# Two layers of linear attention and MLP on one core: settled instruction orders and buffers arranged anew, two tiles transposed by DMA, b1 and b2 loaded later, last tile in 384 + 128 columns

## The chip, the core and the metric

The kernel runs on one core of a Trainium2 chip. A core has five engines with instruction streams of their own: PE (matmuls, and the loading of their weights, PEld), DVE (vector work), ACT (functions of one input, with tables that must be switched between exponential and GELU), POOL (general vector work, slower) and SP, which here only issues DMAs. They wait for each other by semaphores alone. PE writes to PSUM, eight banks of 512 float32 columns by 128 rows; everything else lives in SBUF, 128 rows.

The metric is the device time of a run in microseconds (us), the median of several runs. A few lines of a profiled execution show where it goes.

## The reference

The input is 2048 rows of 512 numbers in bfloat16. Two equal layers follow each other, each a linear attention with 32 heads of 16 and an MLP of width 1792, with residual adds:

```python
def _A_ref(x, wqkv, wo):
    q, k, v = ...                          # x @ wqkv, 32 heads of 16
    phi = lambda t: jnp.where(t > 0, t + 1, jnp.exp(t)) + 1e-6
    pq, pk = phi(q), phi(k)
    kv = jnp.einsum("bhsd,bhse->bhde", pk, v)
    z = jnp.einsum("bhsd->bhd", pk)
    num = jnp.einsum("bhqd,bhde->bhqe", pq, kv)
    den = jnp.einsum("bhqd,bhd->bhq", pq, z)[..., None] + 1e-6
    return (num / den) @ wo                # heads side by side
def _B_ref(x, w1, b1, w2, b2):
    y = _layernorm(x)
    return gelu(y @ w1 + b1) @ w2 + b2
x = x + _A_ref(_layernorm(x), A_wqkv, A_wo)
x = x + _B_ref(_layernorm(x), B_w1, B_b1, B_w2, B_b2)
x = x + _A_ref(_layernorm(x), A_wqkv, A_wo)
x = x + _B_ref(_layernorm(x), B_w1, B_b1, B_w2, B_b2)
```

## The kernel before

The 2048 rows are 16 tiles of 128 rows, in four groups of four. Counting tiles from one, "tile five" is tile 4 in the names. The names in the order lists are those of the code: the first digit behind a letter is the layer, 0 or 1, then the tile or the group and the part.

First stage, for each tile: `norm` (L755) takes mean and variance on DVE (statsA0, aggrA0; for tile 3 by two ACT passes, sumA0_3 and sqA0_3), adds epsilon (vepsA0, DVE or POOL), raises to -1/2 on POOL (powA0) and writes the normalised tile on DVE or ACT (normA0). The tile is then turned, columns to rows, either by `transpose_pe` (L808: four PE instructions PTA0 of 128 columns into a PSUM bank, then a copy tcA0 by ACT) or by `transpose` (L800: one DMA on SP's queue, TA0). `attn_k` makes the keys (K0, four matmuls of 512 columns) and `phi` (L834) their features by an exponential on ACT (expk0), a second pass (reluk0) and work on DVE (mink0) and DVE or POOL (phik0). `attn_g_held` sums tile-transposed times features over all tiles in four PSUM banks (G0), `attn_z` sums the features (Z0, sixteen one-column matmuls for a group), `attn_q` makes the queries (Q0) and their features.

Then V and the output weights are folded into the sum (`attn_kv`: KV0, kvm, M0, cpm), the denominators are made (`attn_den`: D0 with ln and rec on ACT for the first two groups; pz, red, den, rec on POOL and DVE for the other two, with pr multiplying the query features and TP turning them by DMA), and `attn_out` multiplies (WO0) and adds the residual on DVE (RA0). `mlp_front` normalises (normB0), turns the tile (TB0 by DMA) and adds b2 to the residual (b20, POOL or DVE). `mlp_up` makes the hidden layer (W10; group 0 in two halves of 256 columns, the others 512) with GELU on ACT, `mlp_down` sums it (W20, two halves of seven matmuls) and adds the residual (RB0). The second layer does the same with names 1; its key sum goes by groups through `gacc`, its output rows leave by SP's queue (OD). The last tile's down product is made in two column halves (W21_15_h0 and _h1, L1141 to L1159), each with its own PSUM bank, DVE add and output DMA.

Nothing is scheduled when the program is built. `CONF` holds for each engine the whole order of its instructions (ORDER), for each buffer the order in which its tiles use it (PLACES), and for each step that has a choice its way (WAY: which engine, or PE against DMA). `Settled` (L105) takes these, makes every first user of a buffer wait for all users of the tile before it, and `assign_waits` (L186) puts a semaphore wait where an instruction needs one of another engine's. Each engine goes through its list strictly in order. WARM is a list of warm-up blocks at the start of PE's list: matmuls of constants into a PSUM bank, with their columns.

In the order of before, PE starts with 15 warm-ups of 512 columns, then PTA0_0 and PTA0_1, K0_0, PTA0_2, K0_1 and so on. Tiles 0 to 5 are turned by PE, 6 to 15 by DMA. On SP's queue, b2 is loaded between the transposes of tiles 12 and 10, and b1 after the last of them (`dma(..., after=[tr])`, L1193 to L1198, only behind tile 0's transpose by dependence). POOL issues the loads of wv, wo, w1 and w2 once all first-stage transposes are there (`late`, L1205 to L1212).

Of the kernel before, what the change touches and what calls it, by code (L numbers as in the profile page):

```python
# [10 lines left out]
P = 128  # L11
S = 2048
D = 512
# [172 lines left out]
def assign_waits(graph, order, sems, dma_sems):  # L186
# [10 lines left out]
    while len(done) < total:  # L197
        moved = False
        for e in ENGINES:
# [42 lines left out]
    WARM=[[512, 512, 512, 512, 512, 512, 512, 512, 512, 512, 512], [512, 512, 512, 512]],  # L242
# [40 lines left out]
        "act":  # L283
# [1046 lines left out]
```

## Time and profile before

| | us |
|---|---|
| three runs | 328.95, 328.55, 329.53 |
| median | 328.95 |
| the profiled execution | 327.5 |
| its span, first to last instruction | 326.3 |
| granted PE clock in it | 1.000 |

The page of the profile gives the engines' busy time and the chain of work that ended last, followed back from the end. "PE ps L866" is a matmul of line 866 that writes PSUM. In the answers in order of time, a row gives the start, the length and what ran; a bracket at its end tells how long the engine was idle before and what ended that. Rows merge neighbours of one kind, so that "x4" are four instructions. Ends of matmuls are modelled and overlap the next start; the distance of starts is the better measure of their cost.

### The profile page before, as it was taken

How to read it: one execution, taken by the hardware profiler on the slowest of the kernel's cores; microseconds unless marked ns; L12 is line 12 of the kernel's file. 1: busy time of each engine (PE TensorE's matmuls, PEld its weight loads, DVE VectorE, ACT ScalarE, POOL GpSimd, SP SyncE). 2: the span in 40 equal slices, each digit the busy share in tenths (PEclk: the TensorE clock that was granted, in tenths of full speed). 3: DMA queues.
4: the chain of work that ended last, by engine and by line, in shares of the span. 5: the costliest groups of instructions: out<-in, count | busy, mean ns of one | idle time of the engine just before them, and what ended most of it. 6: DMA issues, size and time to landing. Idle time of an engine off the chain costs nothing.

```text
span 326.3 us, 4763 instructions
## 1 busy us (share of the span) xinstructions
PE 322.2 (99%) x1723; PEld 159.3 (49%) x1723; DVE 211.0 (65%) x503; ACT 193.1 (59%) x334; POOL 152.5 (47%) x224
## 2 busy tenths in 40 slices
PE   8999999999999999999999999999999999999997
PEld 3444445576454444444444444458644444444444
DVE  5987679996938685142436899999989983300112
ACT  4988769797661416529673477969833454551600
POOL 5662548588663417300757434783856593100000
PEclk9999999999999999999999999999999999999999
DMA  7355753334012210331011110012034322200102
GB/s 266 120 83 97 219 189 104 105 64 68 16 32 50 54 26 3 80 64 34 0 32 33 34 32 0 19 32 50 17 82 94 69 48 66 64 0 2 64 0 80
DMA packets 46883, 20.37 MB, mean 62 GB/s; under 512 B 41932, under 2 KB 45388, under 8 KB 46860
## 3 DMA queue, kind: packets, MB, share of 16 engines
q1 hardware_dynamic: 44572, 13.00, 18.8%
q0 software_dynamic: 1056, 4.72, 4.5%
q10 hardware_dynamic: 1232, 2.36, 2.0%
q8 instruction: 13, 0.21, 0.3%
q14 instruction: 10, 0.08, 0.1%
HBM read 8.00 MB, written 2.10 MB: 31 GB/s over the span
## 4 chain that ended last, share of the span: by engine, by line
PE 97%; DVE 1%; ACT 1%; issue 0%
PE ps L1127 30%; PE ps L1163 29%; PE ps L1097 9%; PE ps L866 8%; PE ps L883 5%; PE ps L987 4%; PE ps L958 4%; PE ps L896 2%; PE ps L747 2%; PE ps L1150 1%; PE ps L1074 1%; PE ps L1008 1%; PE ps L1031 1%; PE ps L941 1%; PE ps L817 0%; DVE pkb L854 0%
## 5 line engine op out<-in xcount | busy, mean ns | idle before, releaser
L1132 ACT ACTIVATE gT<-ps,b1c 128x512 bf16<-128x512 f32 (+1 forms) x140 | 77.1, 600 | 65.3 <-PE ps L1127 65.0
L1127 PE MATMUL ps<-t,w 128*128 128x512 bf16 (+1 forms) x560 | 102.2, 336 | 0.0
L1163 PE MATMUL ps<-w,gT 128*128 128x512 bf16 x434 | 97.6, 379 | 0.0
L1127 PEld LDWEIGHTS ps<-t,w 128*128 128x128 bf16 x560 | 54.6, 98 | 43.7 <-ACT t L827 0.3
L1163 PEld LDWEIGHTS ps<-w,gT 128*128 128x128 bf16 x434 | 42.5, 98 | 50.4 <-DVE xsb L1169 0.2
L782 POOL TENSOR_TENSOR rstd<-veps,neghalf 128x1 f32<-128x1 f32 x64 | 37.9, 602 | 33.5 <-DVE veps L780 31.4
L837 ACT ACTIVATE eb<-ps 128x512 bf16<-128x512 f32 x64 | 37.4, 614 | 18.3 <-PE ps L866 10.5
L1173 DVE TENSOR_TENSOR outb<-ps,xsb 128x512 bf16<-128x512 f32 x15 | 10.1, 686 | 46.3 <-PE ps L1163 40.3
L773 DVE BATCH_NORM_STATS2 stats<-xsb 128x6 f32<-128x512 f32 x48 | 32.3, 678 | 0.4
L848 ACT ACTIVATE rb<-ps 128x512 bf16<-128x512 f32 x45 | 26.6, 617 | 9.2 <-PE ps L866 8.7
L866 PE MATMUL ps<-wqkv,t 128*128 128x512 bf16 x128 | 31.6, 379 | 0.1
L1097 PE MATMUL ps<-gtb,t 128*128 128x512 bf16 x128 | 31.2, 379 | 0.1
L850 DVE TENSOR_SCALAR eb<-eb 128x512 bf16<-128x512 bf16 x45 | 14.0, 321 | 21.1 <-ACT eb L837 21.1
L1113 POOL TENSOR_TENSOR xsb<-xsb,b2b 128x512 f32<-128x512 f32 x20 | 24.3, 1224 | 6.8 <-ACT yb L790 6.6
L790 ACT ACTIVATE yb<-xsb,nmr,rstd 128x512 bf16<-128x512 f32 x21 | 16.7, 812 | 14.2 <-POOL nmr L787 13.9
L780 POOL TENSOR_SCALAR veps<-mv 128x1 f32<-128x1 f32 x35 | 7.6, 217 | 30.8 <-DVE mv L775 28.1
L1063 POOL TENSOR_TENSOR t<-t,rr 128x512 bf16<-128x512 bf16 x14 | 15.5, 1114 | 13.6 <-DVE rr L1059 12.9
L795 DVE TENSOR_SCALAR yb<-xsb,mv,rstd 128x512 bf16<-128x512 f32 x27 | 16.1, 602 | 8.5 <-POOL rstd L782 8.3
L1051 POOL TENSOR_TENSOR lr<-t,zrow 128x512 f32<-128x512 bf16 x15 | 17.9, 1191 | 5.7 <-ACT zrow L971 4.2
L883 PE MATMUL ps<-wqkv,t 128*128 128x512 bf16 x80 | 19.9, 379 | 0.0
L1097 PEld LDWEIGHTS ps<-gtb,t 128*128 128x128 bf16 x128 | 12.3, 98 | 14.7 <-DVE rr L1059 0.6
L866 PEld LDWEIGHTS ps<-wqkv,t 128*128 128x128 bf16 x128 | 12.0, 98 | 14.9 <-ACT t L827 1.0
(97 smaller groups left out, 373.5 us busy)
## 6 DMA issues: line engine op xcount, KB each, us to landing
w<-in_B_w_dram POOLq DMA_DIRECT2D x4, 896.0 KB, 6.9
out_dram<-outb SPq DMA_DIRECT2D x15, 128.0 KB, 1.9
t<-in_A_x_dram ACTq DMA_DIRECT2D x3, 512.0 KB, 4.6
t<-yb SPq DMA_TRANSPOSE x56, 2.5
wqkv<-in_A_wqkv_dram ACTq DMA_DIRECT2D x1, 512.0 KB, 5.8
wqkv<-in_A_wqkv_dram POOLq DMA_DIRECT2D x1, 512.0 KB, 4.6
wo<-in_A_wo_dram POOLq DMA_DIRECT2D x1, 512.0 KB, 5.5
t<-in_A_x_dram SPq DMA_DIRECT2D x1, 384.0 KB, 3.1
```

The lines of the kernel that those rows point to most:

```text
L773: G.op("dve", lambda e: e.bn_stats(stats[:, s.slot, :], src()), 620, reads=src_keys, writes=[k + "s"], tiles=[s, *src_tiles], name=f"stats ...
L782: G.op("pool", lambda e: e.tensor_tensor(rstd[:, s.slot:s.slot + 1], veps[:, s.slot:s.slot + 1], neghalf[:], op=ALU.pow), 570, reads=[k + ...
L837: G.op("act", lambda e: e.activation(eb[:, et.slot, :], bank(bt), ACT.Exp), 478, reads=[src_key], writes=[f"e{tag}"], tiles=[bt, et], name ...
L848: G.op("act", lambda e: e.activation(rb[:, rt.slot, :], bank(bt), ACT.Relu), 478, reads=[src_key], writes=[f"r{tag}"], tiles=[bt, rt], nam ...
L866: ins = e.matmul(bank(b), lhsT=yTa(yT)[:, dt, k * P:(k + 1) * P], rhs=wqkv[:, dt, D:2 * D], start=(dt == 0), stop=(dt == DT - 1))
L883: ins = e.matmul(bank(b), lhsT=yTa(yT)[:, dt, k * P:(k + 1) * P], rhs=wqkv[:, dt, 0:D], start=(dt == 0), stop=(dt == DT - 1))
L1051: lambda e, r=r, tok=tok: e.tensor_tensor(lr[:, r.slot, :], tok(), zrow[:], op=ALU.mult), 1150 if on_pool else 600,
L1097: ins = e.matmul(bank(wb), lhsT=yTa(pq)[:, kt, k * P:(k + 1) * P], rhs=gtb[:, kt, :], start=(kt == 0), stop=(kt == DT - 1))
L1113: G.op("pool" if on_pool else "dve", lambda e: e.tensor_tensor(xsb[:, st, :], xsb[:, st, :], b2b[:], op=ALU.add), 1120 if on_pool else 600 ...
L1127: ins = e.matmul(bank(b, n), lhsT=w1[:, dt, ft * P:(ft + 1) * P], rhs=yTa(yT)[:, dt, k0 * P:k1 * P], start=(dt == 0), stop=(dt == DT - 1))
L1132: G.op("act", lambda e, ft=ft, b=b, k0=k0, k1=k1, n=n: e.activation(gT[:, g.slot, ft * 512 + k0 * P:ft * 512 + k1 * P], bank(b, n), ACT.Ge ...
L1163: ins = e.matmul(bank(b), lhsT=gT[:, g.slot, ft * 512 + k * P:ft * 512 + (k + 1) * P], rhs=w2[:, ft, :], start=(ft == 0), stop=(ft == FT - 1))
```

## The change

The code changes in four places, and `CONF` is new as a whole.

1. WARM: one block of seven matmuls of 512 columns and ten blocks of 256. PE's order puts five of the ten ahead of the first tile's transposes and five behind, ahead of K0_0.
2. WAY: TA0_4 and TA0_5 from "pe" to "dma"; their PTA0 and tcA0 instructions leave PE's and ACT's lists, and two TA0 join SP's.
3. The DMAs of b1 and b2 and the two POOL instructions of the head mask are made behind the loop over first-stage tiles; the loads now depend on all first-stage transposes, and SP's order has b1, Tb1 and b2 behind the last of them.
4. The last tile's down product is made of columns 0 to 383 and 384 to 511.

ORDER and PLACES are different lists on all five engines. Work moves between DVE and POOL (WAY): of the large sums and products of layer 0, thirteen go from POOL to DVE (b20 of tiles 7, 8, 11, 12, 13; pr0_0_3, pr0_1_2, pr0_2_0, pr0_2_2, pr0_2_3; pz0_2_3, pz0_3_1, pz0_3_3) and six from DVE to POOL (b20 of tiles 2 and 6; pr0_0_2, pr0_1_0, pr0_3_0, pr0_3_1); layer 1 and the small epsilon steps change in the same manner. ACT's order has thirteen switches between the exponential's and GELU's table behind the first, instead of eleven. `norm`, `phi` and `attn_k` get an optional path for a centred tile, which no entry of WAY asks for, so that its code makes no instruction.

```diff
-    WARM=[[512, 512, 512, 512, 512, 512, 512, 512, 512, 512, 512], [512, 512, 512, 512]],
+    WARM=[[512, 512, 512, 512, 512, 512, 512], [256], [256], [256], [256], [256], [256], [256], [256], [256], [256]],
...
         "sp":
-            "x0 x1 wk0 TA0_7 TA0_6 TA0_8 TA0_14 TA0_15 TA0_13 TA0_12 b2 TA0_10 TA0_11 TA0_9 b1 Tb1 TB0_1 TB0_0 TB0_2 TB0_3 "
...
+            "x0 x1 wk0 TA0_4 TA0_5 TA0_6 TA0_14 TA0_7 TA0_10 TA0_8 TA0_12 TA0_13 TA0_9 TA0_15 TA0_11 b1 Tb1 b2 TB0_0 TB0_1 "
...
         "pe":
-            "warm0 warm1 PTA0_0 PTA0_1 K0_0 PTA0_2 K0_1 PTA0_3 K0_2 PTA0_4 G0_0_0 K0_3 K0_4 Q0_0_0 G0_1_0 PTA0_5 Q0_0_1 K0_5 "
-            "G0_2_0 Z0_0 G0_3_0 K0_6 K0_7 K0_8 G0_4_0 Q0_1_2 K0_14 G0_5_0 K0_15 G0_6_0 G0_7_0 Q0_1_0 K0_12 Z0_1 K0_13 K0_10 "
-            "K0_11 K0_9 Q0_1_3 Q0_1_1 Q0_0_3 Q0_0_2 G0_8_0 Z0_3 Z0_2 G0_9_0 G0_10_0 D0_0_0 G0_11_0 G0_12_0 D0_0_2 G0_13_0 "
...
+            "warm0 warm3 warm1 warm10 warm7 warm8 PTA0_0 warm4 warm2 warm9 warm6 warm5 K0_0 PTA0_1 PTA0_2 K0_1 PTA0_3 K0_2 "
+            "K0_3 G0_0_0 Q0_0_1 Q0_0_3 K0_4 Q0_0_0 G0_1_0 G0_2_0 K0_5 G0_3_0 Z0_0 G0_4_0 K0_6 K0_14 Q0_1_2 K0_7 G0_5_0 Q0_1_0 "
+            "G0_6_0 K0_10 K0_12 K0_8 K0_13 G0_7_0 K0_9 Z0_1 K0_15 K0_11 Q0_1_1 G0_8_0 Q0_0_2 Z0_2 Z0_3 G0_9_0 G0_10_0 D0_0_0 "
...
         "dve":
-            "ones statsA0_0 aggrA0_0 vepsA0_0 normA0_0 statsA0_1 aggrA0_1 vepsA0_1 statsA0_2 aggrA0_2 normA0_1 statsA0_4 "
...
+            "ones statsA0_0 aggrA0_0 vepsA0_0 statsA0_1 normA0_0 aggrA0_1 statsA0_2 aggrA0_2 vepsA0_2 normA0_1 normA0_2 "
...
-        "TA0_14": "dma", "TA0_15": "dma", "TA0_2": "pe", "TA0_3": "pe", "TA0_4": "pe", "TA0_5": "pe", "TA0_6": "dma",
+        "TA0_14": "dma", "TA0_15": "dma", "TA0_2": "pe", "TA0_3": "pe", "TA0_4": "dma", "TA0_5": "dma",
...
-                for h in range(2):
+                for h, (c0, c1) in enumerate(((0, 3 * P), (3 * P, D))):
                     hb = b if h == 0 else Tile(psum, f"w{L}_{st}_h", "w")
-                    cs = slice(h * D // 2, (h + 1) * D // 2)
+                    cs = slice(c0, c1)
...
-                if st == 0:
-                    dma("sp", lambda e: e.dma_start(b1r[0:FT, :], B_b1.rearrange("(ft p) -> ft p", p=P)), ["b1r"], name="b1", kb=4,
-                        after=[tr])
-                    dma("sp", lambda e: e.dma_start(b2b[:], bass.AP(B_b2.tensor, B_b2.offset, [[0, P], [1, D]])),
-                        ["b2b"], name="b2", kb=128, after=[tr])
-                    consts()
...
+        dma("sp", lambda e: e.dma_start(b1r[0:FT, :], B_b1.rearrange("(ft p) -> ft p", p=P)), ["b1r"], name="b1", kb=4, after=trs)
+        dma("sp", lambda e: e.dma_start(b2b[:], bass.AP(B_b2.tensor, B_b2.offset, [[0, P], [1, D]])), ["b2b"], name="b2", kb=128, after=trs)
+        consts()
```

PE's end in the two orders, the last lists of DVE and SP:

```
PE before:  W21_9_7 W21_15_h0 W21_11_0 W21_11_7 W21_15_h1
PE after:   W21_15_h0 W21_10_0 W21_10_7 W21_8_0 W21_8_7 W21_9_0 W21_9_7 W21_11_0 W21_11_7 W21_15_h1
DVE before: RB1_10 RB1_8 RB1_9 RB1_11 RB1_15_0 RB1_15_1      SP: OD10 OD8 OD9 OD11 OD15_0 OD15_1
DVE after:  RB1_10 RB1_8 RB1_15_0 RB1_9 RB1_11 RB1_15_1      SP: OD10 OD5 OD8 OD15_0 OD9 OD11 OD15_1
```

More of the change, by code (lines that the diff above doesn't have):

```diff
@@ L783, in norm @@
                  570, reads=[k + "v", "neghalf"], writes=[k + "r"], tiles=[s], name=f"pow{tag}")
+            mean = lambda: stats[:, s.slot, 2:3] if by_act else mv[:, s.slot, 0:1]
+            if centred is not None:
+                yc = Tile(YB, f"yc{tag}")
+                G.op("dve", lambda e: e.tensor_scalar(yb[:, yc.slot, :], src(), mean(), None, op0=ALU.add if by_act else ALU.subtract),
+                     300, reads=[k + "m", *src_keys], writes=[f"yc{tag}"], tiles=[s, yc, *src_tiles], name=f"cen{tag}", lat=40, fast=True)
+                centred.append((yc, f"yc{tag}", s, k + "r"))
             y = Tile(YB, f"y{tag}")
@@ L794, in norm @@
             else:
-                G.op("dve", lambda e: e.tensor_scalar(yb[:, y.slot, :], src(), stats[:, s.slot, 2:3] if by_act else mv[:, s.slot, 0:1],
+                G.op("dve", lambda e: e.tensor_scalar(yb[:, y.slot, :], src(), mean(),
                                                       rstd[:, s.slot:s.slot + 1], op0=ALU.add if by_act else ALU.subtract, op1=ALU.mult),
@@ L832, in yTa, with phi @@
             return t4[:, yT.slot, :].rearrange("p (d s) -> p d s", d=DT)
-        def phi(bt, src_key, dst, dst_key, dst_tiles, tag):
+        def phi(bt, src_key, dst, dst_key, dst_tiles, tag, scaled=None):
             et = Tile(EB, f"e{tag}")
-            G.op("act", lambda e: e.activation(eb[:, et.slot, :], bank(bt), ACT.Exp), 478, reads=[src_key], writes=[f"e{tag}"],
-                 tiles=[bt, et], name=f"exp{tag}", lat=90, table="exp")
-            if eng(f"phi{tag}") == "max":
+            by = (lambda: 1.0) if scaled is None else (lambda: rstd[:, scaled[0].slot:scaled[0].slot + 1])
+            more_tiles, more_keys = ([], []) if scaled is None else ([scaled[0]], [scaled[1]])
+            G.op("act", lambda e: e.activation(eb[:, et.slot, :], bank(bt), ACT.Exp, scale=by()), 478, reads=[src_key, *more_keys],
+                 writes=[f"e{tag}"], tiles=[bt, et, *more_tiles], name=f"exp{tag}", lat=90, table="exp")
+            if eng(f"phi{tag}") == "max" and scaled is None:
                 G.op("dve", lambda e: e.tensor_scalar(eb[:, et.slot, :], eb[:, et.slot, :], 1.0, 1e-6, op0=ALU.min, op1=ALU.add),
@@ L847, in phi @@
             rt = Tile(RB, f"r{tag}")
-            G.op("act", lambda e: e.activation(rb[:, rt.slot, :], bank(bt), ACT.Relu), 478, reads=[src_key], writes=[f"r{tag}"],
-                 tiles=[bt, rt], name=f"relu{tag}", lat=90)
+            G.op("act", lambda e: e.activation(rb[:, rt.slot, :], bank(bt), ACT.Relu, scale=by()), 478, reads=[src_key, *more_keys],
+                 writes=[f"r{tag}"], tiles=[bt, rt, *more_tiles], name=f"relu{tag}", lat=90)
             G.op("dve", lambda e: e.tensor_scalar(eb[:, et.slot, :], eb[:, et.slot, :], 1.0, 1e-6, op0=ALU.min, op1=ALU.add),
@@ L856, in phi, with attn_k @@
                  name=f"phi{tag}", lat=60, fast=not on_pool)
-        def attn_k(L, c, k, yT):
+        def attn_k(L, c, k, yT, key=None, scaled=None):
             st = 4 * c + k
@@ L868, in fn @@
                 return ins
-            G.op("pe", fn, 4 * MM, reads=[f"yT{L}_{st}", "wk"], writes=[f"k{L}_{st}"], tiles=[b, yT],
+            G.op("pe", fn, 4 * MM, reads=[key or f"yT{L}_{st}", "wk"], writes=[f"k{L}_{st}"], tiles=[b, yT],
                  name=f"K{L}_{st}", lat=MM_DRAIN, n=4)
-            phi(b, f"k{L}_{st}", lambda: pkb[:, pk.slot, :], f"pk{L}_{st}", [pk], f"k{L}_{st}")
+            phi(b, f"k{L}_{st}", lambda: pkb[:, pk.slot, :], f"pk{L}_{st}", [pk], f"k{L}_{st}", scaled)
             return pk
@@ L1143, in mlp_down, with fn @@
                 ot = Tile(OUT, f"out{st}")
-                for h in range(2):
+                for h, (c0, c1) in enumerate(((0, 3 * P), (3 * P, D))):
                     hb = b if h == 0 else Tile(psum, f"w{L}_{st}_h", "w")
-                    cs = slice(h * D // 2, (h + 1) * D // 2)
-                    def fn(e, hb=hb, cs=cs):
+                    cs = slice(c0, c1)
+                    def fn(e, hb=hb, cs=cs, n=c1 - c0):
                         for ft in range(FT):
-                            ins = e.matmul(bank(hb, D // 2), lhsT=gT[:, g.slot, ft * 512 + k * P:ft * 512 + (k + 1) * P], rhs=w2[:, ft, cs],
+                            ins = e.matmul(bank(hb, n), lhsT=gT[:, g.slot, ft * 512 + k * P:ft * 512 + (k + 1) * P], rhs=w2[:, ft, cs],
                                            start=(ft == 0), stop=(ft == FT - 1))
                         return ins
-                    G.op("pe", fn, FT * 109.2, reads=[f"g{L}_{c}_{ft}_{k}" for ft in range(FT)] + ["w2"], writes=[f"w{L}_{st}_{h}"],
+                    n = c1 - c0
+                    G.op("pe", fn, FT * (n / 2.4 + 2.5), reads=[f"g{L}_{c}_{ft}_{k}" for ft in range(FT)] + ["w2"], writes=[f"w{L}_{st}_{h}"],
                          tiles=[hb, g], name=f"W2{L}_{st}_h{h}", lat=MM_DRAIN, n=FT)
-                    G.op("dve", lambda e, hb=hb, cs=cs: e.tensor_tensor(outb[:, ot.slot, cs], bank(hb, D // 2), xsb[:, st, cs], op=ALU.add), 340,
-                         reads=[f"w{L}_{st}_{h}", ("x", st)], writes=[f"out{st}_{h}"], tiles=[hb, ot], name=f"RB{L}_{st}_{h}", lat=60)
+                    G.op("dve", lambda e, hb=hb, cs=cs, n=n: e.tensor_tensor(outb[:, ot.slot, cs], bank(hb, n), xsb[:, st, cs], op=ALU.add),
+                         60 + n * 1.06, reads=[f"w{L}_{st}_{h}", ("x", st)], writes=[f"out{st}_{h}"], tiles=[hb, ot], name=f"RB{L}_{st}_{h}", lat=60)
                     dma("sp", lambda e, cs=cs: e.dma_start(rows(out_dram, c)[:, k, cs], outb[:, ot.slot, cs]), [f"od{st}_{h}"],
-                        tiles=[ot], reads=[f"out{st}_{h}"], name=f"OD{st}_{h}", sem=f"d_out_h{h}", kb=64)
+                        tiles=[ot], reads=[f"out{st}_{h}"], name=f"OD{st}_{h}", sem=f"d_out_h{h}", kb=n // 4)
                 return
```

16 lines of the change are left out of this document (12 added, 4 removed), and 486 rows, old and new, of tables (ORDER, PLACES, WAY).

## The prediction

> **What bounds the kernel now.** I read the page first, for the shares, then the busy time by stretches, to see where the engine with the highest share ever pauses, then the chain of work that ended last, in order of time.
>
> ```profile
> span 326.3 us, 4763 instructions
> PE 322.2 (99%) x1723; PEld 159.3 (49%) x1723; DVE 211.0 (65%) x503; ACT 193.1 (59%) x334; POOL 152.5 (47%) x224
> PE 97%; DVE 1%; ACT 1%; issue 0%
> ```
> ```profile
> 0.00:8.00 8.00, 6.96 (x23) 2.61 (x23) 4.42 (x12) 3.39 (x6) 4.56 (x16) 1.00 0.72 264
> 32.00:40.00 8.00, 7.34 (x54) 3.46 (x52) 5.45 (x13) 5.84 (x12) 4.33 (x5) 1.00 0.68 198
> 48.00:80.00 32.00, 32.00 (x204) 19.00 (x202) 28.41 (x67) 28.20 (x54) 24.53 (x29) 1.00 0.40 96
> 240.00:318.00 78.00, 77.87 (x362) 35.17 (x360) 33.20 (x68) 30.38 (x47) 22.44 (x28) 1.00 0.21 50
> ```
>
> The columns of the second view are the stretch, its length, the busy time (and instructions) of PE, its weight loads, DVE, ACT and POOL, PE's granted clock, the DMA engines' share and GB/s. TensorE (PE) is the bound: 97% of the chain, 322.2 of 326.3 us busy, and from 48 to 80 us it doesn't pause at all. Faster work on any other engine buys nothing there. A change of order can only win where PE waits (0.66 us in 32 to 40, 0.13 in 240 to 318), ahead of its first useful matmul, behind its last one, or by taking instructions off PE. It can lose everywhere. The chain shows the two ends and the wait:
>
> ```profile
> 0.84 6.34 PE ps L747 x15
> 7.17 0.24 PE ps L817 x4
> 7.43 0.60 ACT t L827
> 8.09 1.04 PE ps L866 x4
> ...
> 14.28 0.86 PE ps L896 x4
> ...
> 16.00 0.22 PE ps L817 x4
> ...
> 30.82 2.71 PE ps L866 x12
> ...
> 36.16 0.69 DVE pkb L843
> 36.85 1.18 DVE pkb L854
> ...
> 39.16 0.29 DVE eb L841
> 39.45 0.34 DVE pkb L854
> 39.84 0.55 PE ps L941 x16
> ...
> 322.61 1.54 PE ps L1150 x14
> 324.17 0.42 DVE outb L1155
> ```
>
> Four 512-column matmuls take 0.86 us (0.216 each), but the fifteen warm-ups 6.34 (0.42 each): until about 7 us PE runs at half rate, though the granted clock of that stretch reads 1.00.
>
> **The change part by part: the start.** The warm-ups shrink from fifteen of 512 columns to seven of 512 and ten of 256, and five of the ten stand behind the first tile's transposes. The other engines decide what that is worth:
>
> ```profile
> 3.21 0.69 DVE L773 BATCH_NORM_STATS2 stats<-t 128x6 f32<-128x512 bf16 x1 [1.75 <-DMA t<-in_A_x_dram]
> 4.99 0.41 DVE L795 TENSOR_SCALAR yb<-t,mv,rstd 128x512 bf16<-128x512 bf16 x1 [0.68 <-POOL rstd L782]
> 8.34 0.38 DVE L795 TENSOR_SCALAR yb<-t,mv,rstd 128x512 bf16<-128x512 bf16 x1
> 10.35 0.41 DVE L795 TENSOR_SCALAR yb<-t,mv,rstd 128x512 bf16<-128x512 bf16 x1
> ```
> ```profile
> 4.42 0.63 ACT L764 ACTIVATE eb<-t 128x512 bf16<-128x512 bf16 x1 [2.34 <-DMA t<-in_A_x_dram]
> 5.53 0.72 ACT L768 ACTIVATE eb<-t,stats 128x512 bf16<-128x512 bf16 x1 [0.39 <-POOL stats L766]
> ```
>
> Before, tile one is normalised at 5.40 (4.99 + 0.41), and its transposes wait for the warm-ups until about 7. After, the second tile's statistics (0.69, from the landing at 4.42) go ahead of that normalise, so it ends near 5.5. The warm-ups ahead of the transposes end at 0.84 + 7 x 0.42 + 5 x 0.21 = 4.85. PE then idles some 0.65, transposes from 5.5 to 5.95 (0.22 doubled by the half rate), runs the other five (1.05) to 7.0, and the copy on ACT (0.60 from about 6.0) is done by then. The first key product starts near 7.0 instead of 8.09.
>
> Not all of these 1.1 us last. The third tile's normalise moves from 8.34 to about 7.3, but the squares of tile four (0.72) now stand behind the first copy, ahead of the second, which is so ready near 8.75. Second key product 8.8, third 9.9, fourth 10.75, first G product 11.6, then two query products that now stand here (they fill the time in which tile five's transposed block arrives): 7 groups of four done by about 14.35 on the chain's scale, where the chain of before has 6 at 14.28. That is 0.86 - 0.07 = 0.8 ahead. Bounds: 0.3 (the copy of each tile again paces PE as before) and 1.1.
>
> **Tiles five and six by DMA.** Eight PE transposes leave; the first four lie in the count above, the other four are the 0.22 at 16.00. Two copies leave ACT. Two transposes join the SP queue and land on their own:
>
> ```profile
> L804 SPq DMA_TRANSPOSE t<-yb x56: 1188/1265/2193, 15.3 to 278.6; - x56
> DMA to landing us min/median/max: 2.4/2.5/4.3
> ```
>
> Tile five's normalise ends near 10.7 (before: 10.35 + 0.41), so its block is there at 13.3, and its key product stands at 14.2: cover 0.9. At the longest landing (4.3) it would wait 0.9. Tile six: normalised near 14.1 (POOL now builds half a mask ahead of its reciprocal root), landed 16.6, used at 14.2 + 4 x 0.86 = 17.6: cover 1.0. Twelve transposes at 1.27 each keep SP busy for 15 us; begun at 10.7 and waiting for some normalises they end by 24 to 29, and the last block is used by PE 21 groups and a z product behind 14.2, at some 33. I take nothing for the queue and 0.22 for the four transposes.
>
> **b1 and b2.** Their loads leave the middle of the transposes; b1, its transpose and then b2 follow once the last block has landed, near 30. Their users, the first GELU and the adds of b2, stand behind the whole key-value part, near 60 by the count of groups between. Nothing, either way.
>
> ```profile
> wqkv<-in_A_wqkv_dram POOLq DMA_DIRECT2D x1, 512.0 KB, 4.6
> ```
>
> The loads of the late weights now stand on POOL behind one more sum of query features, which is fed by a query product that ends near 35 and done at about 39. The V weights, first of them, would land near 39 + 4.6 = 43.6 and are used near 47 by the count of groups: cover 3. Nothing, and up to a few us if that sum is late by more.
>
> **The wait at 33 to 40.** From 30.82 to 39.84 the chain holds 9.02 us; PE's work in it is 36 matmuls (7.78) and a z product (0.38), so 0.86 is waiting. The last key products feed sums whose second half is late on DVE (the rows 36.16 to 39.45). After, the last key product is followed by a query, a G, a query and a z product, 2.6 + 0.38, and its own path is exponential and relu (0.60 each, ACT's time for 512 columns), minimum (0.29), sum (0.34) and one more 0.69: 2.5 us. So it just fits. I take 0.7 of the 0.86; bounds 0.2 (DVE again spends 1.18 on a sum) and 0.86.
>
> **The last tile.** 256 + 256 columns become 384 + 128: PE's sum stays (0.0555 per 128 columns, by the transposes' 0.22 for four), and the work behind the last matmul shrinks.
>
> ```profile
> 322.65 0.69 DVE L1173 TENSOR_TENSOR outb<-ps,xsb 128x512 bf16<-128x512 f32 x1 [2.71 <-PE ps L1163]
> ```
> ```profile
> out_dram<-outb SPq DMA_DIRECT2D x15, 128.0 KB, 1.9
> out_dram<-outb SPq DMA_DIRECT2D x2, 64.0 KB, 1.7
> ```
>
> 0.42 for 256 and 0.69 for 512 columns make about 0.29 for 128: 0.13 less. But the last full tile's output now leaves only 0.78 us of PE ahead of the end and lands 1.9 after its issue, about when the last piece does. I take 0.1; bounds 0 and 0.3.
>
> **Everything between 40 and 318.** The order is new on all engines, so waits can come up anywhere. Two more switches of ACT's function table and 13 heavy sums and products of layer one that go from POOL to DVE, against 6 the other way, lie beside PE's work. The order of before loses nothing in 48 to 80, 0.13 us in 240 to 318 and 0.66 in 32 to 40; I take 0.4 for the new one, between the last two.
>
> Sum: 0.8 + 0.22 + 0.7 + 0.1 - 0.4 = 1.4 us gained. The profiled execution took 327.5 us (span 326.3, 1.2 around it) and lies 1.45 below the median of the runs, 328.95. It becomes 326.1, and the median 328.95 - 1.4 = **327.5**. With all lower bounds and 0.66 lost: 0.3 + 0.2 - 0.66 and the 0.22, a gain of 0.1; with all upper ones 1.1 + 0.22 + 0.86 + 0.3 - 0.13 = 2.35. The forecast's own range is 326.6 to 328.9.
>
> **Rivals.** *PE stays at half rate.* Before, the rate doubled after 6.3 us of unbroken matmuls. After, they are unbroken for only 4.0 us, then comes a gap of 0.65. For: if the gap restarts the count, the rate doubles near 5.5 + 6.3 = 11.8. Against: within 0.84 to 7.0 PE still works nine tenths of the time. Price: from 7.0 to 11.8 work goes at half rate, 2.4 us of it lost, some 0.9 hidden in the waits for copies: 1.5. Gain -0.1, so 329.05, no change.
> The Trainium skill's page "TensorE: Matmul & The Clock Gate", Part 1, has the rate doubled after one busy window of about 3.4 us, with windows that don't start with the kernel, so that the point varies. The 6.3 us of this trace lie within two such windows. By that rule the doubling may come before 7.0 or after 10, by chance, and the sum would be 1.4 or near nothing.
>
> *DVE becomes the bound in 48 to 80* (the other side). There it is busy 28.41 of 32 us, 89%. Of the moved instructions five of those that join DVE and two that leave it fall into this stretch, net 3 more:
>
> ```profile
> L1113 DVE TENSOR_TENSOR xsb<-xsb,b2b 128x512 f32<-128x512 f32 x12 | 11.9, 999 | 0.0
> ```
>
> At 0.69 to 1.0 each (this group shows that a sum from SBUF takes longer than one from PSUM) they add 2.1 to 3.0: 31.0 us. If DVE keeps its 89%, because its idle time is waits for others, the stretch takes 34.8 us, 2.8 longer. It starts 1.7 earlier, so PE leaves it 1.1 later than before; less 0.1 at the end, plus the 0.4: +1.4, 330.35. It decides once PE's second half of the first four tiles has to wait for its normalised blocks. Counted from the first output product, that half stands 18.4 us later (6 single matmuls, 11 groups of four, 14 half-wide groups, seven matmuls); the DVE instructions up to the second of its normalises, the SP issue and the landing come to about 17.8. The cover is 0.6. Against: the POOL waits that DVE sat through get shorter when POOL has less to do, and the third and fourth tile of that group come earlier in DVE's order.
>
> *Tile five late.* At the longest landing of 4.3, and with tile six behind it, PE waits 0.9 in the start: 328.4. Against: 2.5 is the median, and nothing heavy but weights is loading then.
>
> **How the numbers follow.** Forecast 0.54, half rate 0.16, DVE 0.22, late tile 0.08. This kernel's runs tell a change from none beyond 0.3%, about 1 us: faster means under 327.96, slower over 329.94. The forecast is faster in four of five, the late tile in one of four, half rate in one of four (a part of the price): 0.43 + 0.02 + 0.04, and with the upper half of the start's bounds 0.5. DVE is slower in three of four, half rate in one of eight, the forecast hardly: 0.2. The rest, 0.3, is no change. For eight in ten the range runs from 326.5 to 330.3: it leaves out half of the DVE case and the forecast's luckiest end.
>
> **What would show it.** Right: first key product near 7.0; the z products near 37 without a DVE wait ahead of them; PE full from 40 to 318; one 384-column and one 128-column group at the end with about 0.3 us of DVE behind. Wrong: key products of 1.7 instead of 0.86 us near 8 (half rate); PE idle behind the first residual adds, with DVE as releaser, between 60 and 80; a wait of PE for a transposing DMA near 14.

## The result, and the profile after

| | median | runs | lowest, highest |
|---|---|---|---|
| before | 328.9 us | 4 | 328.55, 329.53 |
| after | 326.11 us | 4 | 325.69, 327.05 |

The ratio is 0.9917, with a 95% interval from 0.9889 to 0.9944: 2.8 us faster. The forecast was 1.4 us faster (327.5), with a range from 326.5. The sign was right, and the gain shows at the start, near 40 us and at the end, where it was forecast; its size was twice the forecast, and just outside the range.

The page of the kernel after, and its busy time by the stretches that the prediction used (columns as there):

```profile
span 325.8 us, 4716 instructions
PE 319.6 (98%) x1686; PEld 159.5 (49%) x1717; DVE 214.5 (66%) x522; ACT 194.3 (60%) x334; POOL 134.6 (41%) x205
PE 93%; ACT 3%; DMA 1%; DVE 1%; issue 1%; SPq 0%
```
```profile
0.00:8.00 8.00, 5.96 (x22) 2.88 (x23) 3.96 (x12) 3.11 (x6) 3.56 (x13) 1.00 0.74 266
32.00:40.00 8.00, 7.87 (x79) 4.22 (x80) 5.93 (x18) 6.02 (x12) 1.19 (x2) 1.00 0.20 47
48.00:80.00 32.00, 31.79 (x197) 18.84 (x200) 29.46 (x73) 27.41 (x52) 24.41 (x30) 1.00 0.55 148
240.00:318.00 78.00, 77.58 (x358) 35.73 (x365) 31.77 (x63) 29.77 (x47) 17.76 (x27) 1.00 0.19 46
```

PE looks less busy than before in 48 to 80 and 240 to 318, but nothing waits there: in this trace matmul records are missing at a regular spacing, and each leaves about 0.05 us that looks idle. The list of PE's waits is the better view. Of this execution it holds three, all in the start; the first column is the sum, then how many and the longest:

```profile
PE ps L825 <- DVE yb L803: 1.2, 1, 1.2
PE ps L749 <- PEq L1331: 0.8, 1, 0.8
PE ps L876 <- ACT t L835: 0.5, 1, 0.5
```

The wait between 33 and 40 (0.66 us on L941 before) is gone, and none came in its place. But this execution is the slowest of its kernel's four: its span is 325.8 us, the others' are 324.4, 324.6 and 325.1. The chain in order of time says why:

```profile
1.25 3.91 DMA t<-in_A_x_dram
5.16 0.02 issue
5.19 0.69 DVE stats L775
5.88 0.32 DVE yb L803
6.20 0.05 issue
6.25 0.61 PE ps L825 x4
6.86 1.07 PE ps L749 x5
7.92 1.71 PE ps L876 x4
...
322.97 0.80 PE ps L1160 x14
323.76 0.02 issue
323.79 0.29 DVE outb L1166
```

The block of x for tiles two to four landed 3.91 us after its issue, at 5.16; before, 3.1 us after. The second tile's statistics, which now stand ahead of the first normalise on DVE, wait for it, so PE's first transposes come at 6.25. PE idles 1.2 us and then still runs at half rate: the first key product takes 1.71 us instead of 0.86. The end is as forecast: 128 columns behind the last matmul, 0.29 us instead of 0.42.

So executions of one kernel differ by more than any single term of the sum: the four runs of after span 1.36 us, and its largest term is 0.8. That set the experiments.

### The profile page after: what moved, and what is told of

It reads as the page before. It is cut to its first block, busy times and chain, and to the rows that moved or that the text cites. A ratio compares the mean times of both kernels' runs of the same rounds, so it can differ in the third digit from the quotient of the medians.

```text
span 325.8 us, 4716 instructions
## 1 busy us (share of the span) xinstructions
PE 319.6 (98%) x1686; PEld 159.5 (49%) x1717; DVE 214.5 (66%) x522; ACT 194.3 (60%) x334; POOL 134.6 (41%) x205
## 4 chain that ended last, share of the span: by engine, by line
PE 93%; ACT 3%; DMA 1%; DVE 1%; issue 1%; SPq 0%
PE ps L1137 30%; PE ps L1174 27%; PE ps L1107 8%; PE ps L876 8%; PE ps L893 5%; PE ps L968 4%; PE ps L997 4%; PE ps L906 3%; DMA t<-in_A_x_dram 1%; ACT eb L847 1%; PE ps L1160 1%; PE ps L1084 1%; ACT L1300 1%; ACT rb L858 1%; PE ps L951 1%
## 5 line engine op out<-in xcount | busy, mean ns | idle before, releaser
L1174 PE MATMUL ps<-w,gT 128*128 128x512 bf16 x425 | 98.6, 379 | 0.5
L1107 PE MATMUL ps<-gtb,t 128*128 128x512 bf16 x121 | 30.5, 379 | 0.4
L1180 DVE TENSOR_TENSOR xsb<-ps,xsb 128x512 f32<-128x512 f32 x16 | 10.9, 683 | 25.1 <-PE ps L1174 25.1
L1123 POOL TENSOR_TENSOR xsb<-xsb,b2b 128x512 f32<-128x512 f32 x14 | 18.0, 1285 | 9.2 <-ACT yb L798 6.8
L1061 POOL TENSOR_TENSOR lr<-t,zrow 128x512 f32<-128x512 bf16 x12 | 14.7, 1224 | 9.0 <-ACT zrow L981 5.1
L860 DVE TENSOR_SCALAR eb<-eb 128x512 bf16<-128x512 bf16 x45 | 12.8, 290 | 6.7 <-ACT eb L847 6.6
```

The lines of the kernel that those rows point to most:

```text
L1107: ins = e.matmul(bank(wb), lhsT=yTa(pq)[:, kt, k * P:(k + 1) * P], rhs=gtb[:, kt, :], start=(kt == 0), stop=(kt == DT - 1))
L1123: G.op("pool" if on_pool else "dve", lambda e: e.tensor_tensor(xsb[:, st, :], xsb[:, st, :], b2b[:], op=ALU.add), 1120 if on_pool else 600 ...
L1174: ins = e.matmul(bank(b), lhsT=gT[:, g.slot, ft * 512 + k * P:ft * 512 + (k + 1) * P], rhs=w2[:, ft, :], start=(ft == 0), stop=(ft == FT - 1))
```

## The experiments

Each run stands beside runs of the kernel before on the same chip. Their median shifts between the chips (328.3 to 329.2 us), so the ratios are to be compared.

**The two kernels again.**

> The kernel before, once more. Theory A (the start differs from execution to execution, and the profiled execution of before had a lucky one): the times spread over 328.5 to 329.5 and a new profile, if its time is near 328.9, has its first residual add (DVE L1102) near 55.8 us instead of 54.5, and as few waits of PE behind 42 us as the first profile. Theory B (the middle differs): the first residual add stays at 54.5 and PE waits 1 us or more somewhere in 48 to 318.

> The changed kernel, once more. Its first profile (327.05, the slowest of four runs) shows key products at half rate until 9.4 us and the block of tiles two to four landing at 5.16 instead of 4.40. Theory A: a run near 325.8 starts its first residual add near 53.0 instead of 54.2, and is otherwise the same. Theory B: the first residual add stays near 54.2 and the difference of 1.2 lies behind it.

Before again: 329.28 us (ratio 0.9999, interval 0.9977 to 1.0022), span 328.8. After again: 325.62 us (0.9914, 0.9887 to 0.994), span 324.3. PE's waits in the second execution of before, with the same columns as above:

```profile
PE ps L1097 <- DMA t<-t: 1.1, 2, 0.9
PE ps L817 <- DVE yb L795: 0.9, 1, 0.9
PE ps L747 <- PEq L1315: 0.8, 1, 0.8
PE ps L941 <- DVE pkb L854: 0.7, 1, 0.7
PE ps L1127 <- ACT gT L1132: 0.2, 1, 0.2
PE ps L866 <- DMA t<-yb: 0.2, 1, 0.2
```

In the first execution, on which the prediction rests, the list of before had only three rows: the 0.8 at the start, the 0.7 near 40 and 0.2 for yb. The second is 2.5 us longer. Its largest new wait is at 253.07, and DVE's rows show where it comes from (the bracket is the idle time before, and what ended it):

```profile
253.07 1.02 PE L1097 MATMUL ps<-gtb,t 128*128 128x512 bf16 x4 [0.89 <-DMA t<-t]
```
```profile
247.73 0.69 DVE L1173 TENSOR_TENSOR outb<-ps,xsb 128x512 bf16<-128x512 f32 x1 [3.28 <-DMA out_dram<-outb]
```

There are two output buffers. DVE stands still until an output has landed (3.28 us here, 1.80 in the first execution), the reciprocals behind it come late, then a transpose, then PE's attention output product. After has another order there and no such wait of PE. Of the two theories for before again, each holds in part: the start is 0.7 later than in the first execution, and 1.8 more are lost behind it. Of those for after again, the first holds: the first residual add comes at 52.73 instead of 54.21, and what follows takes the same time.

**The warm-ups alone, both ways.** Before with the new blocks (the first tile's transposes take another bank), and after with fifteen of 512 ahead of everything:

```diff
-            "warm0 warm1 PTA0_0 PTA0_1 K0_0 ...
+            "warm0 warm3 warm1 warm10 warm7 warm8 PTA0_0 warm4 warm2 warm9 warm6 warm5 PTA0_1 K0_0 ...
```
```diff
-            "warm0 warm3 warm1 warm10 warm7 warm8 PTA0_0 warm4 warm2 warm9 warm6 warm5 K0_0 PTA0_1 ...
+            "warm0 PTA0_0 K0_0 PTA0_1 ...
```

> The kernel before with the new warm-ups alone (seven of 512 and five of 256 columns, the first transposes, five of 256; the first transposes use another PSUM bank). Theory A (most of the gain is the earlier start): 1.0 or more faster than before, 327.9 or less. Rival (the old engine orders behind pace the start whatever the warm-ups): within 0.4 of before, 328.5 to 329.3. Rival (half rate costs more than the earlier start gives): slower than before.

> The changed kernel with the old warm-ups (fifteen of 512 columns, all ahead of the first transposes). Theory A: it loses 1.0 or more of the 2.8 (327.1 or more). Rival (ACT and DVE pace the start): it stays within 0.4 of 326.1.

329.14 us (1.0011, 0.9981 to 1.004), and 326.57 (0.9927, 0.9899 to 0.9954; its profiled span, 324.1, is the shortest of all). The warm-ups bring nothing alone, and the old ones cost after nothing that can be told from noise: its median is 0.95 above that of after again on the same chip, but the intervals of the two ratios overlap nearly whole. The rows of before with the new warm-ups, and of after with the old ones:

```profile
7.15 0.38 DVE L795 TENSOR_SCALAR yb<-t,mv,rstd 128x512 bf16<-128x512 bf16 x1
7.59 0.40 PE L817 MATMUL ps<-idp,yb 128*128 128x128 bf16 x4 [0.78 <-DVE yb L795]
7.82 1.03 PE L866 MATMUL ps<-wqkv,t 128*128 128x512 bf16 x4
```
```profile
5.66 0.39 PE L825 MATMUL ps<-idp,yb 128*128 128x128 bf16 x4
6.74 1.04 PE L876 MATMUL ps<-wqkv,t 128*128 128x512 bf16 x4 [0.69 <-ACT t L835]
```

What sets the start of before is DVE: the second tile's normalise begins at 7.14 to 7.25 in each of its executions, whenever the warm-ups end, and PE's first key product, which stands behind that tile's transposes, starts at 7.8 to 8.1. In after the first key product stands ahead of those transposes, and with fifteen warm-ups of 512 columns, which took 5.00 us in this execution, it still starts at 6.74.

**The wait near 250, and that near 40.** The residual sum that waited gets a place of its own, in a slot of the key-feature pool that is free by then; a second kernel also puts the late sum of key features ahead of a query's minimum:

```diff
-                ot = Tile(OUT, f"out{st}")
+                ot, ob = (Tile(PK, "out2"), pkb) if st == 2 else (Tile(OUT, f"out{st}"), outb)
```
```diff
-            "... mink0_11 minq0_0_3 phik0_11 ...
+            "... mink0_11 phik0_11 minq0_0_3 ...
```

> Before with one edit: the last residual sum of tile three (counted from one) goes to a buffer of its own, the unused first slot of the key-feature pool, and not to the second of the two output buffers; so it no longer waits until the output of tile two has landed. Theory: this wait of DVE (1.80 us in the first profile of before, 3.28 in the second, 2.44 in the one with the new warm-ups) makes the reciprocals behind it late, then a transpose, then an attention output product on PE, which waited 0.13, 1.1 and 0.4 us in these three; most executions lose 0.4 to 1.3 us so. Expected: no wait of DVE for an output's landing ahead of that sum, no wait of PE for a transposing DMA between 240 and 262 us, the median 327.8 to 328.7 against 329.1 of before. Rival one, the wait is an accident of the profiled executions: median within 0.4 of before. Rival two, something else sets the product: PE still waits there for 0.4 us or more.

> The same edit, and on DVE the last sum of key features of the first stage goes ahead of the minimum of a query that waits for ACT; it ended the wait of 0.66 us of PE near 40. Theory: both waits are PE's own, so the gains add: 0.66 earlier sum of the keys' features (41.7 becomes 41.1), median 327.1 to 328.0. The prediction had 0.7 for the wait near 40. Rival: PE meets the next late input within a few us, the first residual add stays at 55.2 and the median is that of the run with the buffer alone.

328.44 us (0.9984, 0.9962 to 1.0007) and 328.52 (0.9977, 0.9952 to 1.0002). DVE no longer waits for an output there. PE's wait is 0.3 in the one profile and none in the other, against 0.1, 1.1 and 0.4 in three executions without the edit. The medians are 0.8 and 0.7 us lower, in the expected range for the first kernel and above it for the second, but both intervals reach to no change, so the runs do not settle the size. The second edit failed: PE still waited 0.5 us near 40, now for ACT's exponential, as its rival had it. And that execution, with a span of 329.2, showed what else goes on in the start:

```profile
10.64 0.40 PE L817 MATMUL ps<-idp,yb 128*128 128x128 bf16 x4 [1.77 <-DVE yb L795]
...
25.06 1.02 PE L866 MATMUL ps<-wqkv,t 128*128 128x512 bf16 x4 [1.31 <-DMA t<-yb]
```
```profile
9.38 0.69 DVE L773 BATCH_NORM_STATS2 stats<-t 128x6 f32<-128x512 bf16 x1 [1.83 <-DMA t<-in_A_x_dram]
10.11 0.18 DVE L775 BATCH_NORM_AGGREGATE mv<-stats 128x2 f32<-128x6 f32 x1
10.20 0.38 DVE L795 TENSOR_SCALAR yb<-t,mv,rstd 128x512 bf16<-128x512 bf16 x1
```

The block of x for tiles five to eight landed at 9.35, not 7.49 as in the first execution. DVE takes tile five's statistics ahead of the third normalise, which so began at 10.20 instead of 8.34. Later a transposed block was 1.31 us late.

**That block made late in both kernels.** Its load is exchanged with that of tiles thirteen to sixteen; a third kernel, of before, also moves the statistics behind the normalises:

```diff
-            "wk1 xc1 xc3 ...
+            "wk1 xc3 xc1 ...
```
```diff
-            "... normA0_1 statsA0_4 aggrA0_4 normA0_2 statsA0_5 normA0_3 ...
+            "... normA0_1 normA0_2 normA0_3 statsA0_4 aggrA0_4 statsA0_5 ...
```

> Before, with the loads of x for tiles five to eight and thirteen to sixteen exchanged on ACT's queue, so that the block of tiles five to eight lands about 1.3 us later (near 9.0 instead of 7.5 to 7.9). Theory: DVE takes the statistics of tile five ahead of the third tile's normalise, so the landing of this block sets the third tile's transposes on PE; executions of before differ by it (7.49 in the first profile, 7.75 and 7.85 in others, 9.35 in the slowest). Expected: third normalise near 9.9 instead of 8.3 to 8.7, PE waits over 1 us for it, first residual add 56.3 to 57.5, median 330.0 to 331.2 against 329.2. Rival, these landings are covered by other waits of the first stage: first residual add 54.5 to 56, median within 0.5 of before.

> After, with the same exchange of loads. Theory: after normalises the third tile ahead of the statistics of tile five, and has a G and two query products ahead of tile five's key product, so the late block costs it less: fourth normalise 9.3 to 9.7 instead of 8.2 to 8.4, PE waits 0 to 0.6 us more, first residual add 52.8 to 53.7, median 325.9 to 326.8. Rival: it loses as much as before does, 1 us or more, median 326.9 or above; then the start of after is no sturdier and the extra gain lies elsewhere.

> The kernel before with the exchanged loads, and on DVE the statistics of tiles five and six behind the third and fourth normalise. Theory: most of what the late block costs is that order; third normalise back at 8.2 to 8.4, fourth near 9.5, first residual add 55.2 to 56.2, median 0.6 to 1.5 below the run with the exchanged loads alone. Rival, the wait only moves to the fifth tile's transposes on PE: first residual add and median within 0.4 of that run.

Before lost: 330.81 us, 1.0068 (1.0028 to 1.0108), with the third normalise at 10.05 and the first residual add at 56.61, both as expected. After: 327.03, 0.9948 (0.9928 to 0.9968), about 0.3% above its other ratios, though the intervals overlap. By the ratios it loses about half as much in time as before does, but more than was expected, and over the bound of the rival (326.9). Its profile shows none of that loss behind the second key product. The block of tiles two to four came late as well (5.44, and 5.16 in the first profile of after); the second key product starts at 10.93 against 10.60 there, and from it to the first attention output product both take 42.34 us. So in this execution the late block of tiles five to eight costs nothing, and what the runs lose stays open. The third kernel took 330.3 (1.0061, 1.0036 to 1.0087), no measurable part of the loss won back, and its first residual add comes at 57.14, later still; as its rival had it, PE met the fifth tile's transposes next:

```profile
12.13 0.40 PE L817 MATMUL ps<-idp,yb 128*128 128x128 bf16 x4 [1.06 <-DVE yb L795]
...
24.26 1.02 PE L866 MATMUL ps<-wqkv,t 128*128 128x512 bf16 x4 [1.06 <-DMA t<-yb]
```

In before PE itself stands in line for tile five; in after it has a G and two query products to do while the DMA turns that tile.

**Tiles five and six back on PE.** The kernel after with both tiles turned and copied as before, in two versions that differ in the PSUM bank of the sixth tile's transposes:

```diff
-            "... K0_3 G0_0_0 Q0_0_1 Q0_0_3 K0_4 Q0_0_0 G0_1_0 G0_2_0 ...
+            "... K0_3 PTA0_4 G0_0_0 Q0_0_1 Q0_0_3 K0_4 Q0_0_0 G0_1_0 PTA0_5 G0_2_0 ...
```
```diff
 first:  psum_4  "... q0_0_3 tpA0_5 k0_14 ...
 second: psum_5  "... q0_0_1 tpA0_5 k0_5 ...
```

> After, with tiles five and six turned on PE and copied on ACT, as before. The prediction's step: the DMA's blocks are there in time, eight PE transposes of 0.055 us each are saved, four of them counted; undoing it costs 0.2 to 0.5 us: first residual add 52.9 to 53.2 against 52.73, median 325.9 to 326.3 against 325.6 to 326.1. Rival, ACT is what the first stage waits for: its two copies more (0.6 each) push every later feature, and the first residual add comes at 53.7 or later, the median at 326.6 or above. Rival, the DMA's blocks were late in the kernel after: the first residual add comes earlier than 52.5.

> After, with tiles five and six turned on PE as in the run before, but with the PSUM bank of the sixth tile's transposes behind a query product that ACT empties by 16.7, not behind one that DVE empties at 21.6 us. Theory: most of the 6 us of that run are its 2.75 us wait for the bank and what follows from it, and the rest is ACT: without that wait the first residual add comes at 53.2 to 55.0, the median at 326.2 to 328.0. Rival, the prediction's step (0.2 to 0.5 for eight transposes and nothing for the two copies): 325.9 to 326.3. Rival, ACT's two copies alone set the first stage: median 329 or above.

The first: 331.18 us, 1.0065 (1.0034 to 1.0097), slower than before. The second: 326.96, 0.9945 (0.9917 to 0.9974). The row that separates them, from the first:

```profile
21.64 0.40 PE L828 MATMUL ps<-idp,yb 128*128 128x128 bf16 x4 [2.75 <-DVE t L856]
```

A transpose on PE needs a bank, and the query product that held this one was emptied by DVE at 21.6. With a bank that ACT empties by 16.7 this wait is gone. What is left is about 0.8 us by the ratios (0.9945 against 0.9914 to 0.9925, the intervals overlap), and 0.6 to 0.9 in the first residual add (55.12, against 54.21 and 54.55 in the two executions of after's start that also had a late second block). The traces divide the 0.9. From the second key product to the first attention output product PE takes 43.24 us in this version and 42.34 in both of those. Of the difference, 0.44 is the eight transposes themselves (0.055 each), 0.21 are two short stalls ahead of them, and 0.33 is one query product that comes late behind a transposing DMA, a wait that executions of after have too (0.1 goes off for a stall that only the other two have).

**b2 back among the transposes.**

```diff
-            "... TA0_12 TA0_13 TA0_9 TA0_15 TA0_11 b1 Tb1 b2 ...
+            "... TA0_12 b2 TA0_13 TA0_9 TA0_15 TA0_11 b1 Tb1 ...
```

> After, with the load of b2 back among the transposes on SP, ahead of those of tiles fourteen, ten, sixteen and twelve. The prediction took nothing for its place: median within 0.4 of after's 325.6 to 326.1, the markers up to the first residual add within 0.3. Rival, the transposes behind it land late as the load takes the engines: PE waits 0.5 us or more for a transposing DMA between 20 and 40 us, and the median is 326.5 or above.

In this kernel the load no longer waits for all transposes either. 326.24 us, 0.9911 (0.9885 to 0.9937): no difference. PE's wait for a transposing DMA (0.68) isn't b2's: the unchanged kernel below had 0.75.

**After again, and with the first normalise ahead of the second tile's statistics.**

```diff
-            "... vepsA0_0 statsA0_1 normA0_0 aggrA0_1 ...
+            "... vepsA0_0 normA0_0 statsA0_1 aggrA0_1 ...
```

> The kernel after, unchanged. So far its executions fall into two groups, near 325.3 to 325.8 and near 326.1 to 327.3, and its profiles too: spans of 324.1 to 324.9 with the block of x for tiles two to four landed at 4.39 to 4.44, of 325.8 with it at 5.16. Theory: the second tile's statistics, which stand ahead of the first normalise on DVE, carry that landing into the start. Expected: median 325.6 to 326.3; if the profile's block lands by 4.5, the first normalise at 5.1 and the first residual add at 52.3 to 53.0; if after 5.0, at 5.7 or later and at 54.0 or later.

> The kernel after, with the first normalise ahead of the second tile's statistics on DVE, as before. Theory: the landing no longer reaches the first normalise, which stays at 5.0; the second normalise comes at 6.9 to 7.3 instead of 6.8 or 7.7; so the early landings lose up to 0.4 and the late ones gain about 1. Expected: first residual add 52.7 to 53.3 at any landing, median 325.2 to 326.0, highest run under 326.8. Rival, the second tile's normalise sets the start: it comes at 7.2 or later, PE waits for it behind the first key product, and the median is 326.2 or above. Rival, the two groups have another cause: highest run 326.9 or above as in the kernel after.

326.28 us (0.9925, 0.9899 to 0.9952; 325.05 to 327.37) and 325.83 (0.9918, 0.9892 to 0.9945; 325.40 to 326.75). In the first the block landed early, at 4.29, and the first residual add came at 53.25, past the expected 53.0, with the wait of 0.75 for a transposing DMA in it. In the second the block landed late, at 5.01, and yet

```profile
5.04 0.41 DVE L803 TENSOR_SCALAR yb<-t,mv,rstd 128x512 bf16<-128x512 bf16 x1 [0.68 <-POOL rstd L784]
5.37 0.69 DVE L775 BATCH_NORM_STATS2 stats<-t 128x6 f32<-128x512 bf16 x1
```

the first normalise stays at 5.04, and the first residual add at 52.62, where executions of after with a late block had 54.2 and later. The second normalise came at 7.45, later than expected. This version beats before. Against after the mechanism is shown by one profile; the time is not separable.

## Why the prediction was right in most of its terms and wrong in its size

The executions side by side, from the traces (us). "Rest" is from the start of the first residual add to the start of the last output sum.

| execution | span | tiles 2 to 4 landed | tiles 5 to 8 landed | late transposed block, PE's wait | first residual add | rest |
|---|---|---|---|---|---|---|
| before, first | 326.3 | 4.40 | 7.49 | 0 | 54.52 | 269.65 |
| before, again | 328.8 | 5.40 | 7.75 | 0.2 | 55.20 | 271.48 |
| before, new warm-ups | 327.7 | 4.94 | 7.75 | 0 | 55.37 | 270.29 |
| before, own buffer | 328.1 | 4.56 | 7.85 | 1.2 | 55.91 | 270.10 |
| after, first | 325.8 | 5.16 | 7.55 | 0 | 54.21 | 269.58 |
| after, again | 324.3 | 4.39 | 7.43 | 0.4 | 52.73 | 269.59 |
| after, fifteen warm-ups | 324.1 | 4.42 | 7.83 | 0 | 52.30 | 269.74 |
| after, once more | 325.0 | 4.29 | 7.30 | 0.75 | 53.25 | 269.73 |

**The start** (forecast 0.8 ahead at 14.35, bounds 0.3 and 1.1). Right in size where the second block lands early, as the prediction's row at 4.42 had it. PE of the kernel after, second execution:

```profile
5.55 0.40 PE L825 MATMUL ps<-idp,yb 128*128 128x128 bf16 x4 [0.68 <-DVE yb L803]
5.78 0.72 PE L749 MATMUL ps<-const-bfloat16-1.0 128*128 128x256 bf16 x5
6.63 1.04 PE L876 MATMUL ps<-wqkv,t 128*128 128x512 bf16 x4
7.51 0.65 PE L825 MATMUL ps<-idp,yb 128*128 128x128 bf16 x8
8.58 1.04 PE L876 MATMUL ps<-wqkv,t 128*128 128x512 bf16 x4 [0.43 <-ACT t L835]
...
14.01 1.03 PE L876 MATMUL ps<-wqkv,t 128*128 128x512 bf16 x4
```

The seventh group of before, first execution:

```profile
14.11 1.03 PE L896 MATMUL ps<-t,wqkv 128*128 128x512 bf16 x4
```

The gap of 0.65 was 0.68; the first two key products came at 6.63 and 8.58 (forecast 7.0 and 8.8), and seven groups were done by 14.01. Counted by starts, as in these rows, before had six done by 14.11, so after was 0.86 + 0.10 = 0.96 ahead. But the reason was in part another. The prediction had the first transposes of before wait for the warm-ups, and gained by shortening them. The two kernels with exchanged warm-ups show that these alone change nothing that can be measured: the new ones leave the first key product of before at 7.82, and with the old ones after has it at 6.74 and seven groups done by 14.11, still 0.86 ahead (its warm-ups took 5.00 us; an execution with the 6.34 of the first of before was not traced there). What gains is the new order of the engines, on PE above all the first key product ahead of the second tile's transposes. That the size came out so well is partly luck. Where the block lands late, 2 us of this go, and 1.5 to 1.9 are still missing at the first residual add (54.21 against 52.73 and 52.30). The prediction saw the order of the two DVE instructions, but took the landing as fixed.

**Half rate as a rival.** It was given 0.16, and it came in the executions with a late block: 1.71 us for the first key product in the first profile. Its condition was right in kind: a gap in PE's work, but a longer one than it took. At 0.4 to 0.7 us of gap the first key product ran at full rate (its row spans 1.04, the last matmul drawn out, where a slow one spans 1.91); in the four executions with 1.1 to 1.5 it did not. By the Trainium skill's page "TensorE: Matmul & The Clock Gate", Part 1, the rate doubles after one busy window of about 3.4 us that does not start with the kernel. The traces agree that the point varies: fifteen unbroken warm-ups took 6.34, 5.77, 5.14, 5.14, 5.02, 5.00 and 4.84 us. By the starts of these matmuls the rate doubled 2.9 to 6.0 us after the first, in three of the seven before 3.4 us of work, where the rule does not have it.

**Tiles five and six by DMA.** The covers were right: tile five's block landed at 13.16 and was used at 14.01 (0.85, forecast 0.9), tile six's landed at 15.92 and was used at 17.46 (1.5, forecast 1.0). The prediction's terms for the eight transposes make 0.44, 0.22 here and as much in its count of the start. Putting them back cost 0.6 to 0.9: the same 0.44, 0.2 of short stalls beside them, and one late transposing DMA. The two copies on ACT were counted at nothing, and PE waits directly for neither in that trace. So the term may be too small by 0.2; a single execution shows it.

**SP's queue** was taken at nothing, and that was wrong by up to 0.75: beside tiles five and six only the last block was given a cover. One transposing DMA took far longer than its median of 2.5 and PE met it, on the chain of the second execution:

```profile
17.66 4.04 DMA t<-yb
21.70 0.14 issue
21.84 1.02 PE ps L876 x4
```

Executions of both kernels have such waits near 21 to 25 us, from nothing to 1.3 us.

**b1, b2 and the late weights**: nothing, as forecast. The V weights landed at 45.41 in the second execution and were used at 47.54: cover 2.1 for the 3 forecast.

**The wait at 33 to 40**: 0.7 was forecast, and the whole 0.66 is gone in every profile of after; the z products stand at 36.9 in the second execution. That a single swap in before only changed what PE waits for fits the prediction's reason, the query and G products in between, but no run tried these alone.

**The last tile**: 0.1 forecast. 0.29 instead of 0.42 on DVE; from the last matmul's end to the end of the span 2.06 instead of 2.12.

**New waits between 40 and 318**: 0.4 was set aside, and none came. "Rest" in the table is the same in after as in the first execution of before. DVE in 48 to 80 rose by 1.05 us (28.41 to 29.46; its rival had 2.1 to 3.0), and PE never waited for it.

**The step that failed** is the last one: "lies 1.45 below the median of the runs ... It becomes 326.1, and the median 328.95 - 1.4". It takes the 1.45 for a constant of both kernels. Execution against execution the sum was near: from 326.26 to 324.34 is 1.9, which is the forecast 1.4, the 0.4 that was not lost, and 0.1 of small misses. But the distance to the median depends on the kernel, and on which execution the profiler caught. The profiled run behind the span of 324.3 took 325.61 us, 0.5 below the 326.11 of after's four runs (and 0.4 below the mean of the six on its own chip), not 1.45; the difference is the other 0.9. The first profiled run of after lay 0.9 above. The table shows it: other executions of before reach the first residual add 0.7 to 1.4 later than the first, and the two without the buffer lose another 0.6 and 1.8 behind it. The late-block versions of before, which are not in the table, lose 0.8 and 1.5 behind it, and of the two with a buffer of their own one still loses 0.45 and the other nothing, while seven executions of after and its variants lie between 269.58 and 269.83. The profile that the sum was made on was before at its best. Averaged over the table, after has its first residual add 2.1 earlier (55.25 to 53.12), where the prediction's first three terms make 1.72, and takes 0.8 less behind it (270.47, without the buffer's row, to 269.66), where the prediction set aside a loss of 0.4. So the misjudged stretch is mainly that between 40 and 318: the order of before loses there in most executions, and the 0.13 of one profile stood for all. Shown are a late x block in the start of before (by making it late) and, by the profiles, the wait near 250. How the 0.9 divides between them and late transposed blocks stays open, since these are few executions and the runs with the buffer alone cannot be told from no change.

## What to carry to other kernels

Where the profiled execution lies below the median by more than the change is worth, find what the other executions wait for before making the sum: each input that lands just in time in the trace can be a wait in some other run, and a new order that gives it cover can gain what no single trace shows. Look at what stands behind a DMA on an in-order engine, both loads and outputs whose buffer is to be used again: moving an instruction that needs nothing from it ahead takes the landing off the path, and the first normalise of after, moved behind such a load, shows the same the other way round. And a matmul or a transpose moved in a settled order needs a PSUM bank of which one knows who empties it, and when.

## What had not been expected of the hardware

The granted clock reads 1.00 in 0 to 8 us of both first profiles, though warm-ups started 0.43 us apart there, and 512-column matmuls start 0.216 apart at full rate. When the rate doubles varies between executions of the same instructions: of fifteen equal warm-ups about all ran slow when they took 6.34 us, and about half when they took 4.84. With a gap of 1.2 us in them it doubled only near 9.6 us.

The same load of 384 KB, issued at the same time, landed 3.0 to 4.2 us later in these executions, and one transposing DMA of the first stage took 4.04 us beside a median of 2.5. A few such landings are worth more than most terms of the sum.
